# A fused linear-attention and mixture-of-experts kernel on one core: block sums held back, a fourth seven-product layer, and a new written order

## The chip, the cores and the metric

The kernel runs on one core of one Trainium2 chip. The metric is device time in microseconds, from launch to end. Seven runs of the kernel before gave a median of 969.24 us (968.5 to 970.36). The engines are TensorE (PE; its weight loads are shown apart as PEld), VectorE (DVE), ScalarE (ACT), GpSimd (POOL) and SyncE (SP); each executes its own instructions in the order in which they were written. SP and POOL issue the DMA transfers that matter here.

## The reference

```python
def phi(x): return np.where(x > 0, x, np.exp(x) - 1.0) + 1.0
q_p, k_p = phi(q), phi(k)                       # (8, 8, 576, 64)
kv  = einsum('bhsd,bhse->bhde', k_p, v)
z   = sum(k_p, axis=2)
x   = einsum('bhsd,bhde->bhse', q_p, kv) / (einsum('bhsd,bhd->bhs', q_p, z) + 1e-6)
x   = x.transpose(0, 2, 1, 3).reshape(4608, 512)
P   = exp(x @ w_gate - max)                     # (4608, 8)
8 times:  P /= P.sum(1) + 1e-9;  P /= P.sum(0) + 1e-9;  P *= 4608 / 8
out = sum over e of P[:, e] * (maximum(x @ w1[e], 0) @ w2[e])   # w1: 512 x 1024, w2: 1024 x 512
```

Attention without a softmax gives 4608 rows of 512. A gate matrix, normalized eight times over rows and over columns (Sinkhorn), weighs eight experts, each of two dense layers with a ReLU between, and all experts work on all rows.

## The kernel before

**The work and its pieces.** The front is the attention. It goes by half batches: `att(b, g)` handles batch b and four of its eight heads, so there are 16 of them, numbered n = 2b + g from 0. Each loads k, q and v (576 KB each, L260; on POOL's queue for n from 2 to 5, on SP's for the others, two buffers of each), takes exponentials on ACT (L273), forms phi on DVE (L277, L282), casts v (`f_v`, L228 on ACT or L230 on DVE), multiplies k by v on PE (L308), scales the product into `kvz` (`f_z`: L318 on ACT, L320 on DVE), transposes q (L335), copies it out (`f_qc`), computes denominators (L350) and numerators (L374), divides (L379), transposes the result (L390) and copies it into `xT` (`f_xc`), the matrix x transposed, in fp16. Each two batches, `logits` multiplies by the gate (L408); after all of them `sinkhorn` runs its chain, mostly on DVE (L431 to L463), and leaves the weights in `P_sb`.

The experts go by groups of 512 rows, `NG` = 9. A unit is one expert and one group. Its first layer is either plain (`layer1`: 8 jobs of 4 matmuls of 512 columns, L550, each with a ReLU on ACT, L554) or in seven products (`block7`): the operands are cut in 2 x 2 blocks, and seven products of sums and differences of blocks replace eight. Each product is 4 matmuls of 256 columns (L665); there are two sets of seven for a unit. Partial results pass through ACT copies (L677, L684, L691), and four results of 128 x 512 a unit are formed on DVE by an add with ReLU (L700), the others by a ReLU on ACT (L694, L697). Seven products need the combinations `W` of w1 (`combos`, L829, 4 DVE instructions) and the four sums of blocks of x (`x_blocks`, L588, 4 DVE instructions of 128 x 512 each for one group).

Expert 0 uses the sums from SBUF. For experts 1 to 7 all of them are read back from DRAM: for every group, `x_blocks` writes the sums (`f_st`, L598, 512 KB) and the raw blocks (`f_raw`, L573 and L574, 128 and 256 KB) to `xd[g]` by SP's queue, and `x_load` fetches 896 KB for each unit. For groups 0 to 4 (`early`, g < `NX` = 5) the sums are formed while the front still runs, in a half of a result buffer that is free then; for groups 5 to 8 they are formed in a pool of two buffers that exists only once the front is closed (`f_close`: all front tasks are done, their memory is given back).

For expert 0 the first `NG - NL` groups have plain first layers, and the last `NL` = 3 (groups 6, 7, 8) have seven products. Its second layers are plain (L771), their results are copied to `acc` (L228 or L230) and, for groups below 8, scaled by `P_sb` once that is known (`f_s`: L798 on ACT, L800 on DVE). Experts 1 to 7 use seven products in both layers (L665 and L889), apart from the last unit's second layer.

**What sets the order.** Nothing is ordered by a loop. Every piece of work is a task handed to a planner (`_Plan`): which engines it may use with a cost for each, what it depends on, which buffers it takes, and a priority. The planner plays the tasks through in simulated time; an engine that comes free takes, of the tasks that are ready, the one with the lowest priority value, and the instructions are written out in that order. A copy that may go to ACT or DVE goes to the one that can start it first, unless its engine is fixed. The dependencies within the planner only shape this order; what an instruction waits for on the chip comes from the data and buffers. At the end a table `ranks` overwrites the priorities of some thousand tasks by number (all of the front, expert 0 and the beginning of expert 1) and fixes the engine of about a hundred. In the table before, 452 values lie near 7, 389 near -90 and 142 near -95, tasks of one kind being spread over all three. Tasks that are not in it keep their own priority; the products of expert 1's first unit start at 7.35. Also in the order: 34 tasks of warm-up matmuls (L481), which run when PE has nothing else in the plan, most before 20 us.

Of the kernel before, what the change touches and what calls it, by code (L numbers as in the profile page):

```python
# [122 lines left out]
def kernel(  # L123
# [43 lines left out]
    NL = 3  # L167
# [69 lines left out]
    gates = {}  # L237

    def fadd(*a, **kw):
        t = add(*a, **kw)  # L240
        front_ids.append(t)
        return t

    def att(b, g):
# [48 lines left out]
        def f_v(e):  # L293
            copy(e, gvv["tile"][:, :, :, 0:D], gin["v"]["tile"])
        tvv.append(fadd({"act": 1.15, "dve": 0.76}, f_v, deps=[ta, tin["v"]],
                        use=[gvv, gin["v"]], prio=pr))
        if n in (0, 15):
            def f_gate(_):
                nc.gpsimd.tensor_copy(out=gate, in_=gin["v"]["tile"][:, 0, 0, 0:4])
            gates[n] = add(("pool", 0.15), f_gate, deps=[tin["v"]], use=[gin["v"]], prio=pr)  # L300
# [10 lines left out]
        tkv = fadd(("pe", 0.6), f_kv, deps=[tph["k"]] + tvv, acq=[gkv], use=[gvv, gt["k"]], prio=pr)  # L311
# [10 lines left out]
        tz = [fadd({"dve": 0.42, "act": 0.52}, f_z, deps=[tkv], acq=[gz], use=[gkv], prio=pr)]  # L322
# [6 lines left out]
        for j0, j1 in ((0, 5), (5, NJ)):  # L329
# [11 lines left out]
            tq.append(fadd({"act": 0.12 + 0.1 * (j1 - j0), "dve": 0.17 + 0.057 * (j1 - j0)}, f_qc, deps=[t1, tqa],  # L341
# [17 lines left out]
        tden = fadd(("pe", 0.35), f_den, deps=tq + tz, acq=[gden], use=[gq, gz], prio=pr)  # L359
# [58 lines left out]
    def sinkhorn():  # L418
# [45 lines left out]
        return add(("dve", 0.8), f_p, deps=last, prio=-200.0)  # L464
# [100 lines left out]
    def x_blocks(g):  # L565
# [10 lines left out]
        for i in range(4):  # L576
# [12 lines left out]
            last = add(("dve", 0.42), f_T, deps=deps + [None if early else t_close, last] + ([xst_of[g - 1][2]] if i == 0 and g > NG - NL else []),  # L589
# [153 lines left out]
    def unit_plain(e, g, gW=None, tW=None):  # L743
# [36 lines left out]
        for tt in range(1 if e > 0 else 0, 4):  # L780
# [21 lines left out]
            if e == 0:  # L802
                tf = add({"act": 0.59, "dve": 0.69}, f_fin, deps=[ty[tt], t_close if g >= NA else None, p_done if g >= NF else None] + (xse_done if g == NA - 1 else []),
                         use=[gy[tt]], prio=g - 400.0)
                if g < NF:
                    tf = add({"act": 0.6, "dve": 0.49}, f_s, deps=[tf, p_done], prio=NG + g - 400.0)
# [176 lines left out]
    for tt in (3, 2, 1, 0):  # L983
# [5 lines left out]
        0:-89.9985 36:7.0644 38:-89.9709 40:7.0686 42:-89.9973 43:-89.9982 44:-89.9988 45:7.0608 46:-94.9754  # L989
        47:7.0659 49:7.056:act 50:7.0719 51:-94.9757 52:-89.9889:act 54:-94.979 55:7.0674:dve 56:-94.979  # L990
        57:7.068:act 58:-89.9808 59:-89.9958 61:-89.9913 62:-89.9922 63:7.062 64:-89.9988 65:-89.9988
        66:-89.9997 67:7.0701 68:-90.0042 69:-94.9772 70:7.0695:dve 71:-94.9724 73:-89.9991 75:7.0641
        77:7.0605 78:-89.9682 79:-90.0003 80:-89.9793 81:7.0692 82:-89.9964 84:7.0635:act 85:7.0662
        86:-94.9715:dve 88:-89.9703 89:7.0509:act 90:-89.9904 91:-89.9865:act 92:7.05 93:7.0647 95:-89.9715
        96:7.0695 97:7.0647 98:7.0659 99:-89.9976 100:7.065 101:-90 102:7.0557:dve 103:-89.9967 104:7.05:act
        106:7.0491 108:7.0713 110:7.0551 112:-89.9967 114:7.0611 116:7.0476 117:7.0503 118:-90.0042
        119:7.0467 120:-89.9958 121:7.0584 123:-94.9751:act 124:-89.9877 125:-90.0036:dve 127:-89.997
        128:-89.991:dve 129:-94.976 130:-89.9943:dve 131:7.0707 132:-90.006 134:7.059 135:7.0707 136:7.065
        137:7.0641 138:7.0575 139:-89.9892 140:-94.9778 141:-89.997:dve 142:-94.9757 143:-94.9775:dve
        144:7.0494 146:7.0632 148:-89.9982 150:7.0617 151:-94.9763 152:-89.994 153:7.0683 154:-89.9841  # L1000
        155:-94.976 157:7.0623:dve 158:7.0635 159:-89.9874 161:-89.9964 162:-89.9949:dve 163:7.0641
        164:-94.9778:act 165:7.068 166:-89.9688 168:-94.976 169:-94.9745 170:-94.9733 171:7.0644
        172:-94.9784 173:7.068 174:-94.9871 175:-90.0141 176:-94.9745 177:7.0653:act 179:-89.9997
        181:-89.9946 183:7.0635 184:-94.9697 185:-89.9985 187:-90.0045 189:7.0641 191:-94.9829 192:7.0671
        193:-89.9925 194:-94.9769 195:7.0731 196:-89.9685 198:7.0647 199:7.0641 200:-89.9895:act
        202:-89.9901 203:-89.985 204:-94.9814 205:-94.9772:dve 206:-90.0156 207:7.0668 209:-94.9781
        210:-94.9808 211:-90.0075 212:-94.9754 213:7.0704 214:7.065 215:-89.9892 216:-94.9841 217:-89.9868
        218:-90.0141 219:-89.9922 221:-94.9766 223:-89.97 225:7.0656 226:7.0584 227:-89.9937 228:7.0641
        229:-94.9754 230:-90.0117 232:-94.9862:act 233:7.0647 234:7.0635 236:7.0713 237:7.068 238:-89.9907
        239:-94.976:dve 240:7.062 241:7.0653 243:-94.9742 244:-90.015 245:-90.0105 246:7.0656 247:7.0425  # L1010
        248:-94.9832 249:-94.9697 250:-94.9796 251:-94.9781 252:-89.9856 253:7.0659 255:7.0641 257:-89.9949
        259:7.065 260:-94.9787 261:-89.9871 262:-94.9781 263:7.0662 264:7.0653 266:-89.9832 267:-94.9799
        268:-89.9901 270:-94.9772 271:7.0698 272:-90.0114 273:-94.9808:act 274:-89.9889 275:-94.9787
        277:-90.0117 278:7.0746 279:-94.9793 280:-94.9757 281:7.0734 282:-94.9799 283:-94.9736
        284:-94.9826:act 285:7.0764 286:-90.0117 287:-94.9802 289:-89.9865 291:-94.9871 293:-90.0138
        294:7.0692 295:-90.0099 296:7.0683 297:7.0668 298:7.041 300:-90.0171:act 301:7.0674 302:-90.0135
        304:-90.0111 305:7.0596:dve 306:7.0434 307:-94.979 308:7.0749 309:7.0668 311:7.0605 312:-90.0129
        313:-94.9757 314:-89.9868 315:-89.9979 316:-89.9877 317:7.0692 318:-89.991:dve 319:-90.0126
        320:-89.9898:dve 321:-89.9934 322:-90.0117 323:-90.0114 325:-90.0132 327:-94.9733 329:-94.9856
        330:7.0668 331:-89.9862 332:7.0665 333:-90.0108 334:7.0671 336:-94.9829:dve 337:-89.9877 338:7.0752  # L1020
        340:-94.9745 341:-90.0132:dve 342:-89.9901 343:7.0656 344:-90.0114 345:-90.0132 347:-89.9916
        348:-90.0117 349:7.0665 350:-90.0159 351:-90.0066 352:-90.0132 353:7.0404 354:-94.9775 355:-89.9964
        356:-90.0108 357:7.0644 359:-94.9829 361:-94.9772 363:-89.9955 364:-94.9763 365:-94.9733
        366:-90.0141 367:7.068 368:7.0743 370:-94.982:dve 371:-94.9781 372:-89.9844 374:-90.0138
        375:-94.9781:act 376:-89.9709 377:-94.9823:dve 378:7.0662 379:-89.9703 381:-89.9883 382:-89.9898
        383:-94.9724 384:-90.006 385:-89.9892 386:-89.9916 387:-90.0093 388:-89.9883:act 389:-89.979
        390:7.0695 391:-94.9826 393:-94.9793 395:-89.9901 397:-90.012 398:7.0656 399:-94.973 400:-89.9724
        401:-90.0144 402:7.0713 404:7.0404:act 405:-89.9871 406:7.0662:dve 408:-89.9898 409:-94.9715:dve
        410:7.0581 411:-89.9883:dve 412:7.0617 413:-89.9868 415:-90.0102 416:7.0707 417:-89.9781
        418:-89.9937 419:-89.9955 420:-89.9901 421:-90.0084 422:-90.0057:dve 423:7.0368 424:7.0617  # L1030
        425:-90.0159 427:-94.9802 429:-90.0105 431:-90.0111 432:-90.012 433:7.065 434:7.0419 435:-90.0075
        436:-94.9802 438:-94.9724:act 439:-90.0123 440:7.041:act 442:-90.0102 443:-89.9973 444:-90.0105
        445:-89.991:act 446:-90.0102 447:-89.9967 449:7.0551 450:-89.9901 451:-89.9871 452:-89.9856
        453:-89.9916 454:7.0701 455:7.0389 456:-89.9676 457:-90.0069 458:-90.0105:dve 459:-94.979
        460:-90.003 461:-90.0111 463:7.0599 465:-90.0078 467:7.0605 468:-90.0123 469:-90.0114 470:-90.0147
        471:7.0677 472:-90.0069 474:-89.9895:dve 475:7.0659 476:7.0548:act 478:-90.0117 479:-90.0108:dve
        480:-89.9949 481:-89.9892 482:7.0659 483:-89.9799 485:7.0545 486:7.0653 487:7.0572 488:7.0734
        489:-89.9946 490:-90.0105 491:-90.0075 492:-89.988 493:-89.9982 494:7.0662:act 495:-94.979
        497:-89.9715 499:7.0419 501:-94.9778 502:-90.0147 503:-89.9886 504:7.0641 505:-89.9955 506:7.0587
        508:-89.9907:act 509:7.0626 510:-90.0087:dve 512:7.0653 513:-89.991:dve 514:7.0671 515:7.0563:act  # L1040
        516:-89.9652 517:7.0767 519:-94.9856 520:-89.9748 521:7.053 522:-89.9955 523:7.0653 524:7.0674
        525:7.0569 526:7.0656:dve 527:-89.9667 528:7.0701:dve 529:7.0665 531:-89.9931 533:-89.9925
        535:-89.9862 536:7.0659 537:-90.003 538:-94.9724 539:7.0647 540:-89.9919 542:-89.9877:dve
        543:-90.0045 544:7.0638 546:-89.9925 547:7.0707:dve 548:-94.9739 549:7.0629:act 550:-89.9967
        551:-94.9724 553:7.0665 554:7.071 555:7.0641 556:7.0656 557:7.0611 558:-89.9673 559:7.0653
# [111 lines left out]
```

## Time and profile before

| what | value |
| --- | --- |
| median of 7 runs | 969.24 us (968.5 to 970.36) |
| the profiled execution | 969.09 us, span 967.3 us |
| granted TensorE clock | 1.000 |
| PE, DVE, ACT, POOL busy | 956.2, 773.8, 570.1, 116.1 us |
| last input (v of half batch 15) lands | 109.57 us |
| last transposes of the front on PE | 133.86 us |
| Sinkhorn chain on DVE, first to last instruction | 137.48 to 182.22 us |
| first seven-product matmul of expert 0 | 143.38 us |
| first second-layer product of expert 1 | about 200 us |

Times within the run are counted from the start of the span. The span is what the profile covers; the run's own time has 1.79 us more around it. PE counts as busy while matmuls are in flight, so its busy share says where work is under way and not how dense it is. For the density the chain of waits is of use: it shows 4 matmuls of 512 columns in 0.86 us and 8 of 256 columns in 0.87 us. In a group's line, "idle before" is the time in which the engine had nothing to run ahead of these instructions, and behind the arrow stands what ended most of it. Idle time of an engine that does not set the end costs nothing.

### The profile page before, as it was taken

The numbers are of one execution on the slowest core, as the hardware profiler recorded it, in microseconds if no ns is written. First come the engines' busy times: TensorE is split into PE (matmuls) and PEld (weight loads), VectorE is DVE, ScalarE is ACT, GpSimd is POOL, SyncE is SP. The second block draws the span as 40 slices with busy tenths as digits, with TensorE's granted clock in tenths as the row PEclk, the third lists the DMA queues.
The fourth block names the chain that finished last, engine by engine and source line by source line (L and its number), as shares of the span: only waits on it lengthen the run. The fifth ranks groups of instructions, "written<-read, shape, count | busy, mean of one in ns | idle before, by whom it ended". The sixth has DMA issues, their size and how long they took to land.

```text
span 967.3 us, 21537 instructions
## 1 busy us (share of the span) xinstructions
PE 956.2 (99%) x8809; PEld 801.4 (83%) x8809; DVE 773.8 (80%) x1532; ACT 570.1 (59%) x1031; POOL 116.1 (12%) x163
## 2 busy tenths in 40 slices
PE   8999999999999999999999999999999999999998
PEld 4566656688888888888888888888888888888886
DVE  6899778988887888878887888878887888877775
ACT  6788645765555555555555555555555555555553
POOL 4100000011111111111111111111111111111110
PEclk9999999999999999999999999999999999999999
DMA  9996942252227222272226322272226322235554
GB/s 316 343 355 242 270 147 100 40 125 77 77 78 162 79 78 78 81 160 77 76 76 126 103 73 72 75 159 74 75 78 138 101 78 78 78 98 164 164 164 110
DMA packets 46420, 121.99 MB, mean 126 GB/s; under 512 B 4208, under 2 KB 18288, under 8 KB 46320
## 3 DMA queue, kind: packets, MB, share of 16 engines
q1 hardware_dynamic: 30576, 96.22, 29.5%
q0 software_dynamic: 15344, 23.87, 12.7%
q8 instruction: 69, 1.13, 0.5%
q10 hardware_dynamic: 400, 0.52, 0.2%
q14 instruction: 31, 0.25, 0.1%
HBM read 119.69 MB, written 17.69 MB: 142 GB/s over the span
## 4 chain that ended last, share of the span: by engine, by line
PE 92%; DMA 4%; ACT 3%; DVE 1%; issue 0%; POOL 0%; SPq 0%; ACTq 0%; POOLq 0%
PE ye L889 33%; PE hq L665 23%; PE att L665 12%; PE Zye L665 6%; PE Zye L889 6%; PE ye L771 5%; PE hq L550 3%; DMA vin<-in_v_dram 2%; DMA kin<-in_k_dram 2%; ACT acc L798 1%; PE kv_ps L308 1%; PE xt_ps L390 1%; PE num_ps L374 1%; PE qt_ps L335 1%; ACT h L554 0%
## 5 line engine op out<-in xcount | busy, mean ns | idle before, releaser
L903 DVE SCALAR_TENSOR_TENSOR acc<-ye,P_sb,acc 128x256 f32<-128x256 f32 x620 | 267.2, 479 | 128.5 <-PE ye L889 128.0
L665 PEld LDWEIGHTS <-W 128*128 128x128 f16 x2112 | 206.6, 98 | 26.9 <-issue 1.4
L889 PEld LDWEIGHTS <-S 128*128 128x128 f16 x1984 | 194.2, 98 | 22.4
L889 PE MATMUL ye<-T,S 128*128 128x256 f16 x1488 | 192.8, 273 | 0.0
L665 PEld LDWEIGHTS <-w 128*128 128x128 f16 x1584 | 155.0, 98 | 20.6 <-issue 0.5
L697 ACT ACTIVATE h<-hq 128x512 f16<-128x512 f32 x132 | 78.7, 597 | 147.2 <-PE hq L665 144.3
L913 POOL TENSOR_TENSOR acc<-acc,st 128x256 f32<-128x256 f32 x124 | 87.5, 726 | 619.8 <-ACT st L910 615.9
L889 PEld LDWEIGHTS <-h 128*128 128x128 f16 x1488 | 145.6, 98 | 16.8
L665 PE MATMUL att<-xs,W 128*128 128x256 f16 x1008 | 151.2, 273 | 0.4 <-ACT s L691 0.4
L665 PE MATMUL hq<-xs,W 128*128 128x256 f16 x1008 | 151.2, 273 | 0.4 <-ACT s L684 0.4
L665 PE MATMUL hq<-xs,w 128*128 128x256 f16 x1008 | 140.9, 273 | 0.3 <-DVE h L700 0.3
L694 ACT ACTIVATE h<-Zye 128x512 f16<-128x512 f32 x132 | 78.8, 597 | 43.4 <-PE Zye L665 43.4
L910 ACT ACTIVATE st<-Zye,P_sb 128x256 f32<-128x256 f32 x124 | 52.1, 471 | 78.3 <-PE Zye L889 78.3
L700 DVE CUSTOM_DVE_ANT_0 h<-att,s 128x512 f16<-128x512 f32 x126 | 86.6, 687 | 12.5 <-ACT s L684 11.9
L684 ACT COPY s<-hq 128x512 f32<-128x512 f32 x126 | 73.6, 584 | 36.2 <-PE hq L665 36.2
L862 DVE TENSOR_TENSOR S<-h 128x1024 f16<-128x1024 f16 x124 | 85.3, 688 | 11.8 <-ACT h L697 11.8
L677 ACT COPY Zye<-hq 128x512 f32<-128x512 f32 x132 | 76.7, 581 | 19.3 <-PE hq L665 19.1
L700 DVE CUSTOM_DVE_ANT_0 h<-hq,s 128x512 f16<-128x512 f32 x126 | 86.6, 687 | 0.1
L771 PE MATMUL ye<-w,h 128*128 128x512 f16 x312 | 76.2, 379 | 0.3 <-DMA w<-in_moe_w_dram 0.3
L665 PE MATMUL Zye<-xs,w 128*128 128x256 f16 x504 | 75.6, 273 | 0.0
L691 ACT COPY s<-att 128x512 f32<-128x512 f32 x126 | 74.5, 592 | 0.0
L889 PE MATMUL ye<-T,h 128*128 128x256 f16 x496 | 64.3, 273 | 0.0
(109 smaller groups left out, 950.6 us busy)
## 6 DMA issues: line engine op xcount, KB each, us to landing
xs<-xd SPq DMA_DIRECT2D x63, 896.0 KB, 4.6
w<-in_moe_w_dram POOLq DMA_DIRECT2D x14, 1024.0 KB, 11.1
out_dram<-acc SPq DMA_DIRECT2D x67, 128.0 KB, 2.4
kin<-in_k_dram SPq DMA_DIRECT2D x12, 576.0 KB, 7.3
qin<-in_q_dram SPq DMA_DIRECT2D x12, 576.0 KB, 6.2
vin<-in_v_dram SPq DMA_DIRECT2D x12, 576.0 KB, 7.1
xd<-acc SPq DMA_DIRECT2D x5, 512.0 KB, 6.0
kin<-in_k_dram POOLq DMA_DIRECT2D x4, 576.0 KB, 13.2
```

The lines of the kernel that those rows point to most:

```text
L665: nc.tensor.matmul(dst[:, p, :], lhsT=lhs(p, c), rhs=rhs(c), start=(first and p == 0 and c == 0), stop=(c == 1), skip_group_check=True)
L677: nc.scalar.copy(out=Zt[1], in_=gX["tile"])
L684: nc.scalar.copy(out=gs2["tile"], in_=gX["tile"])
L691: nc.scalar.copy(out=gs5["tile"], in_=gR["tile"])
L694: nc.scalar.activation(out=hd(0, 0), in_=Zt[1], func=AF.Relu)
L697: nc.scalar.activation(out=hd(1, 0), in_=gX["tile"], func=AF.Relu)
L700: nc.vector._custom_dve(TENSOR_ADD_SAT, out=dst, in0=ps, in1=sb, s0=3.0e38, s1=0.0)
L771: nc.tensor.matmul(gy[tt]["tile"], lhsT=gh["tile"][:, f, ds(P * tt, P)], rhs=gw2["tile"][:, f, :], start=(f == 0), stop=(f == NFT - 1))
L862: nc.vector.tensor_tensor(out=Sx[:, i], in0=a0, in1=a1, op=op)
L889: nc.tensor.matmul(bank(g_)[:, s, :], lhsT=lhs(s, kk), rhs=rhs(kk), start=(new and s == 0 and kk == 0), stop=(kk == 3), skip_group_check=True)
L903: nc.vector.scalar_tensor_tensor(out=dst(), in0=bank(g_)[:, s, :], scalar=P_sb[:, gg, e:e + 1], in1=dst(), op0=ALU.mult, op1=ALU.add)
L913: nc.gpsimd.tensor_tensor(out=dst(), in0=dst(), in1=gst["tile"], op=ALU.add)
```

## The change

Four things change, all in the order and the pieces of the first 230 us or so:

- `NL` is 4: group 5's first layer for expert 0 is in seven products too. `combos` and the sums of groups 5 to 8 come ahead of it.
- In the plan, each sum of an early group g (0 to 4) depends on the landing of v of half batch 10 + g.
- Planner costs are set anew for the k-by-v products, `kvz` on ACT, the q copies, the denominators, the end of Sinkhorn and the scaling on ACT. They describe the work; no instruction changes by them but in place and engine.
- The table `ranks` is another one: 1024 tasks, 626 values near 0.65 and 398 near 9.9, 106 of them with a fixed engine. Again both values are spread over all kinds of task.

```diff
     NXB = 7 * 512
-    NL = 3
+    NL = 4
...
+    v_land = []
...
+        v_land.append(tin["v"])
...
-        tkv = fadd(("pe", 0.6), f_kv, deps=[tph["k"]] + tvv, acq=[gkv], use=[gvv, gt["k"]], prio=pr)
+        tkv = fadd(("pe", 0.54), f_kv, deps=[tph["k"]] + tvv, acq=[gkv], use=[gvv, gt["k"]], prio=pr)
...
-        tz = [fadd({"dve": 0.42, "act": 0.52}, f_z, deps=[tkv], acq=[gz], use=[gkv], prio=pr)]
+        tz = [fadd({"dve": 0.42, "act": 0.63}, f_z, deps=[tkv], acq=[gz], use=[gkv], prio=pr)]
...
-            tq.append(fadd({"act": 0.12 + 0.1 * (j1 - j0), "dve": 0.17 + 0.057 * (j1 - j0)}, f_qc, deps=[t1, tqa],
+            tq.append(fadd({"act": 0.165 + 0.105 * (j1 - j0), "dve": 0.14 + 0.069 * (j1 - j0)}, f_qc, deps=[t1, tqa],
                            use=[gp, gq], prio=pr))
...
-        tden = fadd(("pe", 0.35), f_den, deps=tq + tz, acq=[gden], use=[gq, gz], prio=pr)
+        tden = fadd(("pe", 0.26), f_den, deps=tq + tz, acq=[gden], use=[gq, gz], prio=pr)
...
-        return add(("dve", 0.8), f_p, deps=last, prio=-200.0)
+        return add(("dve", 0.94), f_p, deps=last, prio=-200.0)
...
-            last = add(("dve", 0.42), f_T, deps=deps + [None if early else t_close, last] + ([xst_of[g - 1][2]] if i == 0 and g > NG - NL else []),
+            last = add(("dve", 0.42), f_T, deps=deps + [v_land[NG + 1 + g] if early else t_close, last] + ([xst_of[g - 1][2]] if i == 0 and g > NG - NL else []),
...
-                    tf = add({"act": 0.6, "dve": 0.49}, f_s, deps=[tf, p_done], prio=NG + g - 400.0)
+                    tf = add({"act": 0.72, "dve": 0.49}, f_s, deps=[tf, p_done], prio=NG + g - 400.0)
...
     ranks = """
-        0:-89.9985 36:7.0644 38:-89.9709 40:7.0686 42:-89.9973 43:-89.9982 44:-89.9988 45:7.0608 46:-94.9754
+        0:9.9102 36:0.6482 38:0.6287 40:9.8766 42:9.8706 43:0.6587 44:9.8778 45:0.6446 46:0.6482 47:0.6362
...
```

## The prediction

> **What bounds the kernel now.** I read the page's first two parts, then the busy time by stretch, then the chain of work that ended last, and last the timeline around each stop of TensorE.
>
> ```profile
> span 967.3 us, 21537 instructions
> ...
> PE 956.2 (99%) x8809; PEld 801.4 (83%) x8809; DVE 773.8 (80%) x1532; ACT 570.1 (59%) x1031; POOL 116.1 (12%) x163
> ...
> PE   8999999999999999999999999999999999999998
> ```
>
> TensorE is 99% busy and so bounds the whole. Two things can move the time: fewer or cheaper matmuls, and the 11.1 us in which PE is not busy (967.3 - 956.2). The stretches say where those lie (columns: PE, PEld, DVE, ACT, POOL busy, clock, DMA share, GB/s):
>
> ```profile
> 20.00:30.00 10.00, 8.24 (x76) 4.24 (x76) 9.43 (x19) 9.11 (x13) 4.76 (x6) 1.00 1.10 324
> 30.00:40.00 10.00, 8.83 (x88) 5.21 (x83) 6.00 (x13) 5.03 (x9) 0.72 (x1) 1.00 1.14 344
> 40.00:50.00 10.00, 8.98 (x130) 5.79 (x127) 9.05 (x18) 9.39 (x14) 0.00 (x0) 1.00 1.04 389
> ...
> 75.00:115.00 40.00, 39.96 (x481) 25.60 (x478) 35.28 (x75) 29.90 (x46) 2.25 (x3) 1.00 0.81 265
> 115.00:137.00 22.00, 22.00 (x242) 13.89 (x241) 13.97 (x32) 13.18 (x25) 0.00 (x0) 1.00 0.49 91
> 137.00:182.00 45.00, 45.00 (x311) 29.51 (x308) 40.14 (x104) 24.91 (x46) 0.00 (x0) 1.00 0.31 113
> 182.00:200.00 18.00, 17.15 (x117) 11.19 (x115) 15.11 (x32) 16.93 (x31) 3.19 (x2) 1.00 0.37 64
> ```
>
> The reader sees that PE idles 1.76 us from 20 to 30, 1.17 from 30 to 40, 1.02 from 40 to 50, and 0.85 from 182 to 200; elsewhere after 50 next to nothing. In the same early stretches the DMA share is at its highest of the run (1.04 to 1.14). The chain and the timeline say what PE waited for at 38 and 47:
>
> ```profile
> 32.15 13.54 DMA vin<-in_v_dram
> 45.70 0.52 ACT vv L228
> 46.22 0.54 issue
> 46.76 0.59 ACT h L554
> ```
>
> ```profile
> 37.05 0.76 DVE L277 TENSOR_SCALAR tk<-kin 128x1152 f16<-128x1152 f32 x1 [1.13 <-DMA kin<-in_k_dram]
> ...
> 38.20 0.44 PE L390 MATMUL xt_ps<-ident,xn 128*128 128x128 f16 x5 [0.56 <-DVE xn L379]
> ...
> 47.40 1.02 PE L550 MATMUL hq<-xT,w 128*128 128x512 f16 x4 [1.02 <-ACT h L554]
> ```
>
> Both are head-of-line stops. DVE waits 1.13 us for the k of half batch 4, and the xn that PE needs (L379, from 37.73) stands behind it. ACT's cast of v of half batch 5 starts when that load lands (45.70), and the ReLU that frees PE's bank stands behind it. What else used the DMA engines just before:
>
> ```profile
> 24.93 0.34 SPq L598 DMA_DIRECT2D xd<-acc  x1
> ...
> 25.86 0.47 SPq L574 DMA_DIRECT2D xd<-xT  x1
> ```
>
> Block group 0's sums run on DVE from 22.14 to 24.90, and its three stores (L598, L573 and L574: 512 + 128 + 256 = 896 KB) go out at 25 us, in the middle of the loads that PE is about to wait for.
>
> **The change, part by part.** The sum is made against the profiled execution, 969.09 us (span 967.3 plus 1.79 around it); the median of the runs is 969.24, 0.15 above.
>
> *Group 5's first layer in seven products.* Removed: 8 jobs of 4 matmuls of 512 columns. The chain has one such job as "140.65 0.86 PE hq L550 x4", so 8 x 0.86 = 6.88 us. Added: 2 x 7 products of 4 matmuls of 256 columns; "150.87 0.87 PE att L665 x8" gives 0.435 a product, so 14 x 0.435 = 6.09. The gain on PE is 0.79 us, and as PE has no idle time from 137 to 182, where it would run, I count it whole. The Trainium skill's page "TensorE: Matmul & The Clock Gate", section "Back-to-back issue gap", speaks against this step: it gives a sustained spacing of about 131 ns for 512 columns and 81 ns for 128. By that, 32 matmuls take 4.19 us and 56 take at least 4.54, an estimate of 0.34 us lost, and the forecast would be 967.3. The rows have 215 and 109 ns, and I go by the rows.
>
> Beside PE, DVE trades nothing away and gains 4 add-and-ReLU of 0.687 (L700) = 2.75 us; ACT swaps 8 ReLU of 0.612 (L554) = 4.90 for 10 operations of about 0.59 (L677, L684, L691, L694, L697) = 5.9, so 1.0 more. From 137 to 182 DVE has 4.86 us free and ACT 20.1; that is the cover, and I count both at 0. Without it, 2.75 us of DVE lands on the Sinkhorn chain, whose last row (P_sb, L463) ends at 182.22; bound 0 to +2.75.
>
> *Combinations of w1 and the sums of group 5* existed before (same count of L829 and L588). They now precede group 5's products instead of group 6's. W needs the close of the front, and group 5's sums now lie on PE's way: 4 x 0.68 + 4 x 0.415 = 4.4 us of DVE. Cover: the second layer of group 4 and those products that need neither. I count 0 and keep 4.4 for the rival. The new wait of group 6's first sum for group 5's only orders DVE's queue; the sums of 7 now wait for the products of 5, which PE runs a whole unit earlier: 0.
>
> *Held-back sums.* Groups 0, 1 and 2 had their sums at 22 to 25, 43 to 53 and 69 to 70 us; they move to after the v of half batches 10, 11, 12 (landed at 71.93, 80.09 and 84.53 before); group 3's (90 to 96) stay about where they were, and group 4's (102 to 104) wait for 104.36. DVE gives up 4 x 0.415 = 1.7 us at 20 to 30, where it is 94% busy, and about 5.0 us over 20 to 70, and takes as much from 75 on, where it has 4.72 us free in 40: that nearly fills it, bound 0 to +0.3. In SP's queue three stores a group move past the loads of half batches 6 and later: issues of 0.34, 0.43 and about 0.8 us, 1.6 us of SP each. Loads behind them go out earlier by that much; the loads of 12 to 15 may instead stand behind a store that waits for its sum. Who waits for those is the front's end, PE not before. The loads of half batches 4 and 5 are on POOL's queue, so for them the DMA engines count: 896 KB at 344 GB/s is 2.7 us. The waits of DVE (1.13) and of the ACT cast for these loads then go. What is late next is PE's own stock of work: it has group 0's second layer from 35 us on (second half of w2). I take the idle time from 30 to 50 as gone: 1.17 + 1.02 = 2.2 us. Bounds: 0 (another operand at the head of the same two queues) and all the idle from 20 to 50, 3.95.
>
> *New order and planner costs.* The planner's new values agree with rows: kvz on ACT 2 x 0.379 = 0.76 busy, overlapped 0.61 in the timeline (0.52 becomes 0.63); the qpT copy on ACT 0.702 (0.62 becomes 0.69); the scaling of acc on ACT 0.723 (0.60 becomes 0.72). No instruction changes through them but its place and, for copies, its engine. What the order is worth, the trace cannot show; nearest rows: the stops of 20 to 30 (1.76, PE waits for xT copies and ReLUs on ACT and DVE) and of 182 to 200 (0.85, PE waits for bank copies behind ACT's scalings). I take 0, since neither is tied to something that the diff removes; bounds -2.6 (both gone) and +2.6 (as much again, the size that the same kind of order left here).
>
> Sum: -0.79 - 2.2 = -3.0. 969.09 - 3.0 = 966.1, at the median's offset **966.2 us**.
>
> **The rivals.** *Nothing but the matmuls.* The 30-to-50 stops return elsewhere, because front loads saturate the DMA engines with or without 896 KB (share 1.04 to 1.14). For: w2's second half lands at 35.36 and is waited for too. Against: both stops name one load each. 969.24 - 0.79 = 968.45, no change that can be told (0.2%, 1.9 us, is about what a measurement of this kernel can tell).
>
> *PE runs dry at the front's close (slower).* Before, between the front's last transpose (ends 134.14) and the first seven-product matmul (143.38) PE lived on seven of group 5's plain jobs, 7 x 0.86 = 6.0 us. They are gone; the first block products need the close, and most need the 4.4 us of W and sums plus a DVE step of 0.69. Price if nothing covers it 5.1 us: 969.24 - 0.79 + 5.1 = 973.5, or 971.3 with the 2.2 gained. It decides when fewer than about three plain second-layer jobs (2.6 us) are left at the close. For: DVE is loaded more from 75 on, so the close may not move forward. Against: PE's own front work is unchanged and DVE had 8 us free from 115 to 137.
>
> *Sinkhorn ends later.* The 2.75 us of DVE delay P_sb, and the scalings squeeze PE more: 966.2 + 2.75 = 969.0.
>
> *More than one stop goes.* With the -2.6: 963.6, and down to 962 if the loads' advance also removes the tail of each stop.
>
> **How the numbers follow.** Forecast 0.54 (its own range 964 to 967.2), more 0.13, nothing but the matmuls 0.13, late Sinkhorn 0.05, dry at the close 0.15. Faster by over 0.2% (under 967.3) holds the first two, 0.67; within, 0.18 with the middle ones; slower (over 971.2) 0.15. The range 962.0 to 971.8 leaves out the far ends of the "more" and the "dry" cases.
>
> **What would show it.** Right: PE idle from 30 to 50 near 0.3 us; no store of xd before about 75 us; k of half batch 4 and v of 5 landing 2 us earlier than 37.03 and 45.68; 8 fewer groups of four L550 and 14 more products at L665 in PE's rows; PE without idle from 125 to 150. Wrong: idle of the same size at 20 to 60 behind another load or copy; a gap at L665 right after the close, waiting for W or xst; P_sb later than 182 with PE waiting for ACT's bank copies after it. The forecast fails if the order inside ACT's and DVE's queues, and not the DMA load, sets those early stops.

## The result and the profile after

The changed kernel takes 967.11 us (median of 15 runs, 965.45 to 968.43), the kernel before 969.49 (35 runs): a ratio of 0.9972, 95% interval 0.9965 to 0.9978. That is 2.4 us less; the forecast was 966.2, 3.0 less. The profiled execution took 968.18 us, with a span of 966.1.

The page, its first two parts (engine, busy time, share; then the span in 40 slices):

```profile
span 966.1 us, 21596 instructions
...
PE 957.5 (99%) x8833; PEld 804.5 (83%) x8833; DVE 774.5 (80%) x1535; ACT 572.2 (59%) x1033; POOL 113.6 (12%) x163
...
PEclk9999989999999999999999999999999999999999
```

The clock line is new: in the sixth slice the granted TensorE clock (the share of its full rate at which TensorE was let run) is below 1; the mean over the run is 0.996. In the profile before it was 1.000. The stretches (PE, PEld, DVE, ACT, POOL busy, clock, DMA share, GB/s):

```profile
20.00:30.00 10.00, 8.72 (x86) 4.42 (x84) 7.75 (x13) 9.84 (x14) 4.31 (x6) 1.00 1.18 303
30.00:40.00 10.00, 8.86 (x79) 5.23 (x78) 6.97 (x14) 6.11 (x11) 0.82 (x2) 1.00 1.05 385
40.00:50.00 10.00, 10.00 (x114) 6.10 (x112) 9.81 (x21) 9.66 (x15) 0.00 (x0) 1.00 1.00 354
...
75.00:115.00 40.00, 40.00 (x439) 24.49 (x437) 35.48 (x76) 31.96 (x54) 1.82 (x3) 1.00 0.80 267
115.00:137.00 22.00, 21.73 (x320) 15.48 (x318) 15.75 (x37) 9.19 (x19) 0.00 (x0) 0.90 0.78 195
137.00:182.00 45.00, 44.98 (x319) 31.52 (x318) 38.70 (x100) 26.23 (x50) 0.00 (x0) 0.97 0.21 73
182.00:200.00 18.00, 18.00 (x128) 12.30 (x127) 16.59 (x33) 17.29 (x32) 1.64 (x2) 1.00 0.42 87
```

PE's idle time from 20 to 200 us falls from 5.13 to 2.71. Of it, 40 to 50 and 182 to 200 are now without a gap, 20 to 30 has 1.28 (1.76 before), 30 to 40 has 1.14 (1.17 before, but with another cause), and 115 to 137 has 0.27, which is new. No group's blocks are stored before 72 us. The k of half batch 4 lands at 34.23 (37.03 before) and the v of 5 at 41.87 (45.68).

What remains from 30 to 40, in the timeline:

```profile
32.58 1.02 PE L773 MATMUL ye<-w,h 128*128 128x512 f16 x4 [0.87 <-DMA w<-in_moe_w_dram]
...
37.82 0.38 PE L392 MATMUL xt_ps<-ident,xn 128*128 128x128 f16 x4 [0.23 <-DVE xn L381]
```

The stops behind k of half batch 4 and v of half batch 5 are gone; PE now waits 0.87 us for w2's second half, which lands at 32.54. And this is where the clock falls:

```profile
128.69 0.72 PE L392 MATMUL xt_ps<-ident,xn 128*128 128x128 f16 x10
129.69 1.04 PE L410 MATMUL lg_ps<-wg_sb,xT 128*128 128x8 f16 x36 [0.27 <-DVE xT L230]
130.59 0.59 PE L523 MATMUL Zye<-warm 128*128 128x512 f16 x2
131.01 2.92 PE L410 MATMUL lg_ps<-wg_sb,xT 128*128 128x8 f16 x108
133.79 1.87 PE L667 MATMUL hq<-xT,w 128*128 128x256 f16 x8
135.45 1.06 PE L667 MATMUL att<-xst,W 128*128 128x256 f16 x4
136.30 1.06 PE L667 MATMUL hq<-xst,W 128*128 128x256 f16 x4
```

The new table puts all four sets of gate products (L410, 144 matmuls of 8 columns) in one stretch at the front's end, with only two wide matmuls (L523) behind the first set; before, they stood at 48, 90, 111 and 136 us. From 132.7 us, for 6.8 us, the granted clock is 0.5: the first block products follow each other at 0.86 us for 4 matmuls (135.45, 136.30) in place of 0.435. The mean clock is on record for 16 runs, one more than the median counts: it is 0.999 or 1.000 in five, which took 965.45 to 965.55 us, and 0.996 to 0.998 in eleven, which took 966.6 to 968.43.

### The profile page after: what moved, and what is told of

It is laid out like the page before. It is cut to its first block, busy times and chain, and to the rows that moved or that the text cites. A ratio compares the mean times of both kernels' runs of the same rounds, so it can differ in the third digit from the quotient of the medians.

```text
span 966.1 us, 21596 instructions
## 1 busy us (share of the span) xinstructions
PE 957.5 (99%) x8833; PEld 804.5 (83%) x8833; DVE 774.5 (80%) x1535; ACT 572.2 (59%) x1033; POOL 113.6 (12%) x163
## 4 chain that ended last, share of the span: by engine, by line
PE 97%; DMA 2%; DVE 1%; issue 0%; ACT 0%; ACTq 0%
PE ye L891 33%; PE hq L667 24%; PE att L667 12%; PE ye L773 7%; PE Zye L667 6%; PE Zye L891 6%; PE hq L552 3%; DMA w<-in_moe_w_dram 1%; DMA kin<-in_k_dram 1%; PE yw L483 1%; PE num_ps L376 1%; PE xt_ps L392 1%; PE kv_ps L310 1%; PE qt_ps L337 1%; PE lg_ps L410 0%; PE den_ps L352 0%
## 5 line engine op out<-in xcount | busy, mean ns | idle before, releaser
L667 PEld LDWEIGHTS <-W 128*128 128x128 f16 x2144 | 210.7, 98 | 27.4
L667 PEld LDWEIGHTS <-w 128*128 128x128 f16 x1608 | 157.8, 98 | 21.5 <-issue 0.5
L702 DVE CUSTOM_DVE_ANT_0 h<-att,s 128x512 f16<-128x512 f32 x126 | 86.5, 687 | 11.0 <-ACT s L686 11.0
L702 DVE CUSTOM_DVE_ANT_0 h<-hq,s 128x512 f16<-128x512 f32 x126 | 86.6, 687 | 0.1
L891 PE MATMUL ye<-w,h 128*128 128x256 f16 x496 | 64.3, 273 | 0.0
```

Of the source, the lines that this page charges most:

```text
L667: nc.tensor.matmul(dst[:, p, :], lhsT=lhs(p, c), rhs=rhs(c), start=(first and p == 0 and c == 0), stop=(c == 1), skip_group_check=True)
L702: nc.vector._custom_dve(TENSOR_ADD_SAT, out=dst, in0=ps, in1=sb, s0=3.0e38, s1=0.0)
L891: nc.tensor.matmul(bank(g_)[:, s, :], lhsT=lhs(s, kk), rhs=rhs(kk), start=(new and s == 0 and kk == 0), stop=(kk == 3), skip_group_check=True)
```

## The experiments

Two questions were to be settled. Did the stops from 30 to 50 us go because 896 KB of stores left the loads' way (the theory of the forecast), or because the order changed? And is the half clock made by the gate products in one stretch? All kernels but the last two keep the written order of the kernel that they start from and move a few pieces after the plan is made, so that nothing else in the order is drawn along.

### Group 0's stores alone, later

```diff
     # after the plan: tasks 637 and 639 are group 0's stores, 645 is group 1's
+    late = [S_.t[i]["fn"] for i in (637, 639)]     # their own turns become empty
+    S_.t[645]["fn"] = run_with(S_.t[645]["fn"], late)
```

> The kernel before, in its own order, with one thing moved: block group 0's three stores to DRAM (896 KB) are issued on SP ahead of group 1's (about 53 us) and no longer at 25 us; its sums stay at 22 to 25 us. Theory (the 896 KB delay the loads of half batches 4 and 5): k of half batch 4 lands near 34.3 us and v of 5 near 42 to 43 us (37.03 and 45.68 before), PE's stops at 38.2 and 47.4 go, 1.5 to 2.2 us less, about 967.4. Rival (the stops are set by the order in DVE's and ACT's queues): the loads may land earlier but PE stops for as long in 30 to 50 us, time within 0.4 us of before.

Measured: 971.25 us, ratio to before 1.0017 (1.0008 to 1.0026). The loads land at 34.09 and 42.53. Stretches 30 to 40, 40 to 50 and 60 to 75 of this kernel, and from its timeline what PE and DVE waited for at 62:

```profile
30.00:40.00 10.00, 9.88 (x104) 6.17 (x103) 8.05 (x17) 7.13 (x11) 0.72 (x1) 1.00 1.11 382
40.00:50.00 10.00, 9.92 (x133) 6.16 (x132) 9.81 (x20) 10.00 (x18) 0.00 (x0) 1.00 1.05 390
...
60.00:75.00 15.00, 11.49 (x110) 6.39 (x109) 11.60 (x23) 7.97 (x12) 0.00 (x0) 0.89 0.81 288
```

```profile
62.04 0.76 DVE L277 TENSOR_SCALAR tk<-kin 128x1152 f16<-128x1152 f32 x1 [4.05 <-DMA kin<-in_k_dram]
```

```profile
63.54 0.40 PE L374 MATMUL num_ps<-kvz,qpT 128*128 128x128 f16 x4 [3.51 <-DVE rden L356]
```

In the kernel before, the stretch from 60 to 75 and DVE's wait at the same load are:

```profile
60.00:75.00 15.00, 14.71 (x158) 8.77 (x156) 13.93 (x29) 11.95 (x19) 0.00 (x0) 1.00 0.90 320
```

```profile
61.96 0.76 DVE L277 TENSOR_SCALAR tk<-kin 128x1152 f16<-128x1152 f32 x1 [0.82 <-DMA kin<-in_k_dram]
```

The first half of the theory holds: the loads come 2.9 and 3.2 us sooner, and PE's idle time from 30 to 50 falls from 2.19 to 0.20. But 1.8 MB of stores now go out from 48.4 to 52.6 us, just ahead of the k of half batch 9. That k is sent at 54.55 and lands at 62.02 (55.59 and 61.94 before) while the rest has moved ahead: DVE stands 4.05 us at that load, and PE 3.51 us behind DVE. That the stores are what holds this load shows in the kernel of the section "The holding back alone, in the old order", whose order differs here only by these stores and the sums: there it is sent at 51.40 and lands at 57.12, and DVE, which is at the same point 0.4 us later, does not wait for it. The stop is followed by 3.4 us at half clock from 63.8 us (0.89 in the stretch). The gain is not hidden; it is paid back at the next load.

### Group 0's sums later as well

```diff
+    late = [S_.t[i]["fn"] for i in (633, 634, 635, 636)]   # group 0's sums, ahead of 641, group 1's first
```

> As the run with group 0's stores moved, and group 0's four sums on DVE (1.66 us at 22 to 25) moved as well, ahead of group 1's first sum (43 us). Theory that the DMA bytes matter: the same time as with the stores alone, within 0.4 us. Rival that DVE's time at 20 to 30 us (94% busy) matters as much: a further 0.5 to 1.6 us less, and less idle on PE from 20 to 30.

In this kernel group 0's sums come to lie in the same half of the buffer as group 1's and are overwritten, so that group 0's blocks for experts 1 to 7 are not the reference's; the work is the same in amount. Measured: 970.14 us (ratio 1.0011, 1.0003 to 1.0020). From 20 to 30 PE is busy 8.39 us here and 8.94 with the stores alone moved, so no gain from the 1.66 us of DVE shows in that stretch; but profiles of one and the same order differ there by half a microsecond (8.24, 8.49 and 8.77 in the kernel before and in two experiments below that keep its order up to 48 us). Where the sums run now, from 41.4 us on, they cost something: PE idles 1.21 us from 40 to 50 (0.08 with the stores alone), and the stop at 63 us is 2.13 in place of 3.51. The two medians differ by 1.1 us and their intervals overlap. Whether DVE's time at 20 to 30 is worth anything stays open.

### The holding back alone, in the old order

```diff
+    at(649, (633, 634, 635, 636, 641, 642, 643, 644))   # groups 0 and 1: sums at group 2's place
+    at(653, (637, 639, 645, 647))                       #   and their stores
+    at(657, (649, 650, 651, 652, 657))                  # group 2: at group 3's place
+    at(661, (653, 655, 661))
```

> The kernel before, in its own order, with the holding back alone: the sums and stores of groups 0 and 1 moved to group 2's place (69 to 71 us), group 2's to group 3's (90 to 96 us). Theory (with the stores out of the loads' way until most loads are in, the early stops go and nothing replaces them): PE idle from 30 to 50 us at most 1.2 us by issue times (3.57 before), no stop of 3.5 us at 63 us, 1.7 to 2.4 us less than before, about 967.4. Rival (the delay is only handed on: 1.8 MB of stores at 71 us delay the loads of half batches 11 and later, and 3.3 us of DVE in one piece delay the front): new stops between 70 and 100 us, time within 0.5 us of before or longer.

Which half of the buffer a group's sums take goes by the group's number in this kernel, so that none are overwritten. Measured: 969.15 us, ratio 0.9997 (0.9988 to 1.0006). Stretches of this kernel, and the timeline at the two largest of the new stops:

```profile
30.00:40.00 10.00, 10.00 (x121) 6.46 (x113) 7.77 (x17) 7.29 (x11) 0.72 (x1) 1.00 1.12 377
40.00:50.00 10.00, 9.79 (x138) 6.08 (x133) 9.10 (x17) 9.91 (x18) 0.00 (x0) 1.00 1.04 380
...
75.00:115.00 40.00, 38.27 (x461) 24.46 (x460) 35.28 (x76) 27.68 (x43) 2.38 (x3) 1.00 0.83 277
```

```profile
80.88 0.39 PE L374 MATMUL num_ps<-kvz,qpT 128*128 128x128 f16 x4 [1.06 <-ACT qpT L228]
```

```profile
94.80 0.38 PE L335 MATMUL qt_ps<-ident,tq 128*128 128x128 f16 x4 [0.65 <-DVE xn L379]
```

PE's idle time from 30 to 50 falls from 2.19 to 0.21 us and rises from 0.04 to 1.73 from 75 to 115. The rival of this run is right: the old order, written for sums at 22 and 43 us, hands the time on. Between 75 and 115 the forecast had given the moved sums a price of 0 to 0.3.

### The same bytes back into the changed kernel

```diff
+    # once the four xT copies of batch 0 are written out:
+    nc.sync.dma_start(out=scratch[:, 0:2048].rearrange("p (c t) -> p c t", c=4), in_=xT[:, :, 0:512])
+    nc.sync.dma_start(out=scratch[:, 2048:3584].rearrange("p (c t) -> p c t", c=3), in_=xT[:, 0:3, 0:512])
```

> The changed kernel with 896 KB of x, as much as one block group's stores, also written to a DRAM buffer that nothing reads, on SP's queue at about 22 to 25 us, where the kernel before wrote group 0. Theory (these bytes delay the loads of half batches 4 and 5): k of half batch 4 lands near 36.9 us (34.23 in the changed kernel), v of 5 about 2.5 us later than 41.87, idle of PE from 30 to 50 up by 1 to 2.4 us, the time 0.8 to 2.4 us longer. Rival (the early stops were of the order, and this order does not have them): loads later, idle unchanged within 0.4 us.

Measured: 970.58 us, ratio to before 1.0009 (1.0001 to 1.0018), so 3.5 us above the changed kernel's 967.11. k of half batch 4 lands at 37.43, v of 5 at 44.99. The stretches 20 to 40 and the wait:

```profile
20.00:30.00 10.00, 8.29 (x52) 3.69 (x50) 6.75 (x11) 8.06 (x11) 3.70 (x5) 0.83 1.09 321
30.00:40.00 10.00, 7.78 (x88) 4.83 (x87) 4.75 (x12) 5.52 (x10) 1.42 (x2) 1.00 1.14 336
```

```profile
35.99 1.02 PE L773 MATMUL ye<-w,h 128*128 128x512 f16 x4 [2.18 <-DMA w<-in_moe_w_dram]
```

The bytes cost the changed kernel 1.08 us more idle time from 30 to 40 and 0.23 from 40 to 50, at w2's second half and not at k or v. That half lands at 35.95 in place of 32.54, and PE starts on it at 35.99 in place of 32.58: 3.4 us later, about as much as the whole loss. As idle time this counts for less, because the clock falls to a half for 3.4 us from 24.0 and PE is longer at the matmuls ahead of the wait; what the clock costs there, the wait hides. The loss is over the 0.8 to 2.4 expected because all of the delay of this one load reaches PE. Holding the stores back is worth its time in this order: without it, the whole gain is gone.

### Does PE's time count whole near 160 us?

```diff
+                    if first and e == 0 and g == 7:
+                        for _ in range(8):
+                            nc.tensor.matmul(dst[:, 0, :], lhsT=warm[:, 0:P], rhs=warm[:, 0:256], start=True, stop=True)
```

> The kernel before with 32 matmuls of 256 columns on zeros added in group 7's seven-product first layer of expert 0, near 160 us: 32 x 0.109 = 3.49 us of PE. Theory (PE is the bound there, so that PE time counts one for one, as the 0.79 us of group 5's products was counted): 3.2 to 3.6 us more, about 972.9. Rival (PE's stock of work hides part of it, or Sinkhorn's end at 182 us sets the pace): less than 2 us more.

Measured: 972.7 us against 969.58 beside it, ratio 1.0032 (1.0019 to 1.0044), 3.1 us for 3.49 us of work and just under the 3.2 to 3.6 expected, with no idle time on PE from 137 to 182 in either. The interval, 1.8 to 4.3 us, leaves room for a part that is hidden; to that accuracy PE is the bound there, and what is saved there is saved.

### The gate products together, in the kernel before

```diff
+    late = [S_.t[i]["fn"] for i in (183, 184, 321, 322, 459, 460)]   # three sets and their exponentials
+    S_.t[598]["fn"] = run_with(S_.t[598]["fn"], late)                # ahead of the fourth set
```

> The kernel before with the gate products of the first three batch pairs (36 matmuls of 8 columns each) moved from 48, 90 and 111 us to just ahead of the fourth set at 136 us, as the changed kernel has them: 144 small matmuls in one stretch of about 3.5 us. Theory (such a stretch makes the clock gate halve TensorE's clock): a stretch of several us at half clock begins within 4 us of them, mean clock 0.996 to 0.998 in most runs, and the time rises by 1.2 to 3 us. Rival (the half clock in the changed kernel has another cause, for example its block products so early): clock 1.000 and the time within 0.5 us of before.

Measured: 972.77 us, ratio 1.0032 (1.0019 to 1.0044); the mean clock was 0.997 or 0.998 in four of five runs, which took 972.39 to 973.74, and 1.000 in one, which took 970.88. The timeline of its profile:

```profile
135.96 3.80 PE L408 MATMUL lg_ps<-wg_sb,xT 128*128 128x8 f16 x144
139.62 1.87 PE L771 MATMUL ye<-w,h 128*128 128x512 f16 x4
141.28 2.33 PE L550 MATMUL hq<-xT,w 128*128 128x512 f16 x8
```

The clock is 0.5 from 138.8 for 3.4 us, 2.8 us after the first small matmul; four matmuls of 512 columns then take 1.66 us (139.62 to 141.28) in place of 0.86. So the stretch of small matmuls is enough, in another order. The run at full clock is 1.4 us above before all the same: from 50 to 115 PE now idles 2.15 us (0.33 before). The gate products had filled gaps there at no cost.

### The gate products apart, in the changed kernel

```diff
+    for mm, at, ex, then in ((183, 727, 184, 304), (321, 779, 322, 389), (459, 831, 460, 585)):
+        ahead(at, [mm])        # one set of gate products ahead of a second-layer job
+        ahead(then, [ex])      # its exponential a little later
```

> The changed kernel in its own order, with the first three sets of gate products moved ahead to about 54, 83 and 117 us (each in front of plain second-layer matmuls); the fourth stays at the front's end. Theory (144 small matmuls in one stretch halve the clock): no stretch at half clock, clock 0.999 to 1.000 in all runs, 965.5 us or up to 0.7 less, against 967.1 for the changed kernel. Rival (another cause): clock 0.996 to 0.998 as before the move and 967 us.

Measured: 969.61 us, ratio 1.0001 (0.9992 to 1.0010). The clock is 0.999 or 1.000 in all eleven runs, as the theory has it, but the time is 2.5 us longer than the changed kernel's. From the waits of its PE, 30 to 200 us (in total, times, longest):

```profile
PE cs_ps L448 <- DVE h L702: 1.3, 1, 1.3
PE att L667 <- DVE W L831: 1.1, 1, 1.1
...
PE lg_ps L410 <- DVE xn L381: 0.7, 1, 0.7
PE lg_ps L410 <- DVE xT L230: 0.5, 1, 0.5
PE lg_ps L410 <- DVE qpT L230: 0.2, 1, 0.2
```

At their new places the sets wait 1.4 us, each for a PSUM bank (a buffer for PE's results, here of a pool of two) that DVE has to free. And at the front's end PE waits 2.4 us for DVE: 1.1 for the combinations W, and 1.3 for an add with ReLU (L702) that stands in DVE's queue behind W and Sinkhorn's first sums. In the changed kernel the four sets covered just these 4 us of DVE work. Against its runs at full clock, about 965.5, the loss is 4.1 us, and the two kinds of wait make 3.8 of it. This is the forecast's slower rival, PE dry at the close, with a price of 2.4 us; the bunch of gate products is what kept it away.

### The gate products mixed with block products

```diff
+    ahead(598, [853])          # group 5: first m1, ahead of the second set
+    ahead(459, [867, 854])     # the other m1, ahead of the third; the copy that m2 needs
+    ahead(183, [857])          # the first m2, ahead of the fourth
```

> The changed kernel with its order kept but for 12 block products' matmuls on PE: the first products of group 5 (two times m1 and one m2, 4 matmuls of 256 columns, 0.436 us each) are set between the four sets of gate products at 130 to 134 us, so that no two sets of 36 small matmuls follow each other. The sum of PE's work and the cover for DVE's work after the front stay. Theory (a stretch of 3.5 us of small matmuls alone halves the clock): clock 0.999 to 1.000 and 965.5 us in all or nearly all runs, against 967.1. Rival (0.44 us of block products in each 1.3 us is too little for the clock gate): clock 0.996 to 0.998 and 967 us in most runs.

> The changed kernel with the first block products set between the gate products, once more, on the same chip as the changed kernel itself in the same call. Theory (the bunch of small matmuls halves the clock, and the mixing prevents it): clock 0.999 to 1.000 in most runs, 965.5 to 966.2, 0.7 to 1.8 us less than the changed kernel beside it. Rival (the earlier difference was between chips): the two medians within 0.4 us.

> The changed kernel itself, beside its mixed version on the same chip. Theory: a mean clock of 0.996 to 0.998 in over half of the runs and 0.999 to 1.000 in the rest, the former 1.1 to 3 us longer; median near 967.1. Rival (the lower clock was that chip's): clock 1.000 throughout and 965.5.

Measured: 966.1 us (ratio 0.9965, 0.9951 to 0.9978), and again 966.47 (0.9973, 0.9961 to 0.9984) beside the changed kernel itself with 967.32 (0.9977, 0.9967 to 0.9986) on the same chip. The mean clock was 0.999 or 1.000 in nine of the twelve runs of the mixed kernel and in two of the ten of the changed kernel beside it (in seven of 26 with the runs of the result); the latter two took 965.76 and 965.91, the other eight 966.81 to 968.24. The stretch in the second profile of the mixed kernel:

```profile
129.99 1.04 PE L410 MATMUL lg_ps<-wg_sb,xT 128*128 128x8 f16 x36 [0.27 <-DVE xT L230]
130.89 0.59 PE L523 MATMUL Zye<-warm 128*128 128x512 f16 x2
131.32 0.60 PE L667 MATMUL hq<-xT,w 128*128 128x256 f16 x4
131.75 1.04 PE L410 MATMUL lg_ps<-wg_sb,xT 128*128 128x8 f16 x36
132.66 0.60 PE L667 MATMUL hq<-xT,w 128*128 128x256 f16 x4
133.09 1.04 PE L410 MATMUL lg_ps<-wg_sb,xT 128*128 128x8 f16 x36
```

Three block products of 0.44 us between the sets keep the clock at 1.00 through this stretch, and DVE's cover stays. The mixed kernel is the fastest of all here in both comparisons, by 1.0 and 0.85 us under the changed kernel; the intervals overlap, so that the step in the clock is shown and the size of the gain is not settled. The mixing seems to have a small price of its own: at full clock the mixed kernel took 966.23 to 966.48 on the chip where the changed kernel took 965.76 and 965.91.

### One part with the old table

```diff
     # the holding back alone: the plan's new dependency, old costs, old table
+            last = add(("dve", 0.42), f_T, deps=deps + [v_land[NG + 1 + g] if early else t_close, last] + ...
     # the fourth seven-product layer alone, the old table renumbered
-    NL = 3
+    NL = 4
```

> The kernel before with the plan's new dependency alone (sums of early group g after the v of half batch 10 + g), the old table of priorities and the old costs; the planner works out a new order from them. Theory (a table of nearly equal priorities is fitted to one list of tasks and dependencies, and does not carry over): many places in the order change and PE idles far more than before, over 5 us longer. Rival (the part stands by itself): 967 to 969.

> The kernel before with four instead of three seven-product first layers alone; the old table is renumbered so that each task keeps its value, group 5's products take those of group 6's. Theory (the table is fitted to its list of tasks): over 5 us longer, PE idle somewhere between 130 and 200 us. Rival (the part stands by itself): 0.79 us less, about 968.4.

Measured, one run each: 995.42 and 982.67 us, 26 and 13 above before. In the first, PE waits 8.4 us for DVE inside Sinkhorn:

```profile
PE cs_ps L448 <- DVE gs L443: 8.4, 3, 4.1
```

In the second it waits 6.5 us at the same place. Both also run at half clock for a while, 20.5 us in all in the first and 13.7 us from 139.0 us in the second. The likely reason is in the table, though it was only argued: its values within a class differ by a few hundredths and decide ties all over the front, so that with one dependency changed other tasks meet and another order falls out. The new table, dependency and layer were made together, and a part of the change set into the old table says nothing on the part.

## Why the prediction was right, and where it was not

The time fell as forecast and lies within the range and, by 0.1 us, within the likeliest case's own range. The total is nearer than its terms, and that is in part luck: one term was over a microsecond too large, one that was counted at 0 made up for it, and one that the sum lacked took 1.6 us back.

*Group 5's seven products, -0.79.* Both sides of the term stand in the profile: 32 matmuls fewer at L552 and two more sets of seven products. That PE's time counts whole there was shown with padding (3.1 of 3.49 us). Here the first products of group 5 run at half clock in most executions, which the term did not hold. The sustained spacing of the Trainium skill's page "TensorE: Matmul & The Clock Gate", section "Back-to-back issue gap", by which this part would have cost 0.34 us, does not fit the rows: 0.86 us for four matmuls of 512 columns, 0.435 for four of 256.

*The stops of 30 to 50, -2.2.* The mechanism was right and the size too large. The bytes delay the loads (k of half batch 4 by 2.8 us, forecast 2.7), and moving them takes away nearly all of the idle time there in the old order (to 0.20). In the changed kernel 1.14 remain, so by idle time the term is -1.05. The step that failed is the one from "what is late next", where the second half of w2 is named, to idle time that is gone. That half comes at 32.54 now (35.36 before), and PE waits 0.87 us for it. From 30 to 40 this is the sign of being wrong that the prediction gave, idle of the same size behind another load. (That this half "is waited for too" in the kernel before was misread: the 0.32 us of wait for w2 there, at 31.64, are for the first half, landed at 31.59, and PE starts on the second at 35.41 without idle time.) And the step took it that time gained early stays gained; in the old order it came back at 63 us or from 75 to 115.

*The order, 0 within -2.6 to +2.6.* By the idle time of the two profiles it was worth -1.6: -0.29 from 9 to 20 and -0.48 from 20 to 30, -0.29 from 60 to 75, -0.85 from 182 to 200, and +0.27 from 115 to 137. The part from 20 to 30 does not stand. A second profile of the changed kernel has 2.24 us of idle time there, where the first has 1.28 and the kernel before 1.76; the other stretches agree within 0.1:

```profile
20.00:30.00 10.00, 7.76 (x79) 4.03 (x78) 7.54 (x12) 9.60 (x14) 4.08 (x6) 1.00 1.18 304
```

That leaves about -1.2. The order is also what keeps the time gained at 30 to 50. Which of its places does so was not taken apart: the old table with the dependency alone is 26 us off.

*The sum.* -0.79 - 1.05 - 1.2 = -3.0, or -3.4 with 20 to 30 as the first profile has it; the five runs at full clock, about 965.5, are 3.6 under the kernel before's profiled 969.09 and 4.0 under its median of 969.49, so that some tenths are not accounted for. The changed kernel's median lies 1.6 above those five runs. That is the term that the forecast lacked: TensorE's clock.

*The rivals.* Dry at the close came to 0.27 us of idle time before the gate products, because these covered 4 us of DVE; with them moved it is 2.4 us. Sinkhorn ends earlier than before (P_sb at 180.66, before 182.22), not later. The case in which the loads' advance is only handed on is what the old order does with the holding back alone.

## What to carry to other kernels

Here, time won early on a path of many engines was handed on where the order behind it was not made for it; so measure a moved transfer at the next stop as well as at the one it was to cure. Look at what small work covers before it is gathered or spread: the gate products filled PE's gaps at no cost in one order and hid 4 us of DVE work in the other. And look at the clock line of the profile even where PE shows no idle time.

## What the hardware showed

A PE row that is busy without a gap can lose its clock. 144 matmuls of 8 columns, issued every 25 ns for 3.5 us, led to a clock of 0.5 some 3 to 4 us after the first of them (2.8, 3.0 and 4.0 in three profiles), for 3.4 us or 6.8 us; in other kernels of this study the spells were 3.4, 6.8, 10.2 and 13.7 us, all close to multiples of 3.4. Whether it happens differs from run to run of one kernel, and costs it 1.1 to 3 us. The Trainium skill's page "TensorE: Matmul & The Clock Gate", section "Part 1: The HAM clock gate", has a window of about 3.4 us that runs freely, with half clock after an idle window; the lengths and the changes from run to run agree with it. What the runs add is that small matmuls back to back can let the clock fall as idle time does, that 0.44 us of 256-column matmuls in every 1.34 us were enough to keep the clock in nine runs of twelve, and that waits of 3.5 and of 2.1 us in the middle of a run were followed by such a spell too (3.4 us from 63.8 and from 63.9 us, with group 0's stores moved and with its sums moved as well).
